# Imaginary column parts paired one frequency on, evictions of 642 columns on their own partition half, and a new order for the whole kernel

## The chip, the cores and the metric

One core of a Trainium2 chip. The time is device microseconds (us) of one execution, the median over several runs; the runs of one kernel agree within some tenths of a per cent. Of the kernel before, one execution was also taken by the hardware profiler, and all durations below come from it.

## The reference, cut to what matters

```python
xn = _layernorm(x, axis=-1)                 # x: 1 x 2048 x 640, bf16
# A: 2-D real Fourier transform, product with a filter W (2048 x 321), inverse transform
X = rfft2(xn, axes=(-2, -1)) * (w_r + 1j * w_i)
y = irfft2(X, s=(2048, 640)).astype(bf16)
# B: bilinear gated unit, 640 -> 1536 -> 640
h = (xn @ w_gate) * (xn @ w_up)
out = x + y + h @ w_down
```

## The kernel before, in words

Both branches run interleaved on one core. Work is cut into some 970 tasks, each a short list of instructions for one engine, and the order of all tasks is written out as a table, `_PLAN`: rows of (task number, engine, first PSUM bank or -1). `replay` walks the table, appends each task to its engine's list and adds, where a task takes PSUM banks, a dependence on the tasks that emptied those banks before. `compute_waits` turns dependences into semaphore waits. So each engine runs its list strictly in order, and nothing moves at run time. PSUM is eight banks of 512 f32 columns; a task takes a "single" bank or a "pair".

The stages, by the names that the tasks carry:

- **Layernorm** of 16 row groups (`bn`, `ag`, `sm`, `sq`, `sd`, `rs`, `mul`), and transposes: `T0` with evictions `eT0` for the first four groups, the DMA queue for the others.
- **Gated unit**: `GU_f_b_u` is five matmuls of 512 columns (line 940; smaller ones at line 960) for block f of 128 features, row group b, and u = gate or up. `eG` evicts the bank to bf16, mostly on ScalarE (ACT), and `H` multiplies the two on VectorE (DVE, line 976).
- **Forward transform along columns**: `S1` to `S5` on DVE (lines 852 to 887) do butterflies over five, `R_b` (line 900) the first factor along the 2048 rows, and `eR` evicts into buffer `U`, laid out as [contraction, part k, 2048] with column 64 q + m for row frequency q = 0 to 31.
- **D, C, WM, IA**, for t = 0 to 15, each t holding the frequencies q = 2t and 2t + 1. `D_t_w` (line 1017), w = 0 for the real and w = 1 for the imaginary part, is five matmuls of 64 or 65 columns with 128 columns of `U` as weights, so that PSUM partitions 0 to 63 hold q = 2t and 64 to 127 hold q = 2t + 1. `eD_t_w` copies the two halves, 64 partitions x 321 columns each, to `A[64 w + ..., slot, 324 g + ...]`, g = 0 or 1 for the two q: real parts in partitions 0 to 63 and imaginary parts in 64 to 127, so half of the copies change their partition half. `C_t` (line 1037) contracts over those 128 partitions with table `tf`; `WM_t` (six DVE instructions, lines 1054 and 1060) multiplies by the filter, `NS_t` on GpSimd (POOL) negates and copies a part, and for each odd t `SM_t` (lines 1081 and 1082), `JA_t` and `JB_t` (lines 1090 to 1093, on ACT or DVE) combine four frequencies. `IA_q` (lines 1108 and 1110) starts the inverse transform and `eIA_q` evicts it into `Z2`.
- **Inverse**: `I_a` (line 1139), `eI_a`, the butterflies `V1` to `V5` (lines 1163 to 1196), and `IV` (line 1228), which adds into the bank where `ACC` (line 1216) has summed h @ w_down. `FINA` on ACT and `FIN` on DVE add x, and the SP queue stores.

The first 68 us hold layernorm, S, most of R and a little over half of the gated unit; from 71 us D, C, WM and IA run between the rest of the gated unit; from 135 us I, V and the second product.

Buffer `A` has three slots (ar = t mod 3), buffer `Y5` three, `PR` two. All copies that ACT or DVE may do go through one helper, whose two lines the profile names for most of them: 683 (ACT) and 684 (DVE).

Of the kernel before, what the change touches and what calls it, by code (L numbers as in the profile page):

```python
# [255 lines left out]
def _build_tables():  # L256
# [66 lines left out]
    for q in range(_NQ):  # L323
        k = _rows(q, npm, nk1)
        ph = two_pi * ((s1[:, None] * k[None, :]) % _S) / _S
        c = np.exp(-1j * ph)
        pm = np.broadcast_to(npm[None, :], (64, 64))
        f = np.where(ck == 1, np.where(pm == 1, -1j, 1j), 1.0 + 0j)
        if q == 0:
            f = (ck == pm).astype(np.complex128)  # L330
        fm = c * f
        im = (np.conj(c) * f / _S).T
        tf[0:64, q, n_re] = fm.real
        tf[0:64, q, n_im] = fm.imag
        tf[64:128, q, n_re] = -fm.imag
        tf[64:128, q, n_im] = fm.real
        ti[n_re, q, 0] = im.real
        ti[n_im, q, 0] = -im.imag
        ti[n_re, q, 1] = im.imag
        ti[n_im, q, 1] = im.real  # L340
    t["tf"] = _bf16_bits(tf)
# [34 lines left out]
def _d_mm(n):  # L376
    return max(n, 64) / 2.4 + 2.5
# [22 lines left out]
def _d_act(n):  # L400
# [4 lines left out]
    (11, 4, -1), (0, 1, -1), (12, 4, -1), (170, 1, -1), (169, 4, -1), (18, 2, -1), (17, 2, -1), (171, 4, -1), (26, 2, -1),  # L405
    (10, 0, 0), (19, 2, -1), (8, 3, -1), (27, 2, -1), (20, 1, -1), (21, 2, -1), (172, 4, -1), (28, 2, -1), (22, 2, -1),
    (29, 1, -1), (23, 0, 2), (9, 0, 4), (13, 4, -1), (14, 4, -1), (30, 2, -1), (24, 1, -1), (31, 2, -1), (32, 0, 6),
    (33, 1, -1), (25, 2, -1), (173, 4, -1), (34, 2, -1), (181, 0, 5), (179, 0, 4), (189, 0, 0), (35, 2, -1), (174, 4, -1),
    (36, 2, -1), (37, 2, -1), (186, 0, 1), (184, 0, 2), (182, 1, -1), (191, 0, 3), (180, 1, -1), (183, 2, -1), (196, 0, 6),
    (194, 0, 7), (187, 2, -1), (175, 4, -1), (43, 1, -1), (38, 1, -1), (176, 4, -1), (15, 4, -1), (44, 1, -1), (39, 2, -1),  # L410
    (45, 1, -1), (185, 2, -1), (40, 2, -1), (177, 4, -1), (188, 2, -1), (41, 0, 1), (190, 1, -1), (46, 2, -1), (192, 1, -1),
    (42, 1, -1), (47, 2, -1), (193, 2, -1), (199, 0, 5), (195, 1, -1), (197, 1, -1), (178, 4, -1), (48, 0, 4), (112, 2, -1),
    (49, 1, -1), (200, 1, -1), (201, 0, 2), (202, 1, -1), (198, 2, -1), (113, 2, -1), (203, 2, -1), (1, 4, -1), (16, 4, -1),
    (204, 0, 0), (206, 0, 1), (205, 1, -1), (114, 2, -1), (62, 1, -1), (216, 0, 0), (207, 1, -1), (63, 1, -1), (50, 2, -1),
    (217, 1, -1), (54, 2, -1), (53, 2, -1), (51, 2, -1), (115, 2, -1), (64, 1, -1), (52, 2, -1), (55, 2, -1), (2, 4, -1),
    (211, 0, 3), (116, 2, -1), (56, 1, -1), (3, 4, -1), (57, 2, -1), (214, 0, 2), (209, 0, 7), (4, 4, -1), (208, 2, -1),
    (119, 0, 4), (65, 1, -1), (212, 1, -1), (221, 0, 6), (219, 0, 3), (66, 1, -1), (210, 1, -1), (58, 2, -1), (120, 1, -1),
    (60, 2, -1), (121, 2, -1), (215, 1, -1), (213, 2, -1), (222, 1, -1), (122, 2, -1), (117, 0, 0), (72, 1, -1), (218, 2, -1),
    (67, 2, -1), (220, 1, -1), (73, 1, -1), (5, 4, -1), (123, 2, -1), (224, 0, 7), (6, 4, -1), (225, 1, -1), (7, 4, -1),
    (74, 1, -1), (68, 2, -1), (226, 0, 4), (229, 0, 5), (223, 2, -1), (70, 2, -1), (231, 0, 2), (124, 2, -1), (227, 1, -1),  # L420
    (75, 1, -1), (236, 0, 3), (234, 0, 4), (76, 1, -1), (228, 2, -1), (230, 1, -1), (125, 2, -1), (239, 0, 5), (59, 4, -1),
    (61, 4, -1), (77, 2, -1), (78, 2, -1), (69, 4, -1), (232, 1, -1), (80, 2, -1), (82, 1, -1), (71, 4, -1), (241, 0, 2),
    (237, 1, -1), (235, 1, -1), (83, 1, -1), (240, 1, -1), (118, 1, -1), (84, 1, -1), (233, 2, -1), (246, 0, 3), (130, 2, -1),
    (126, 0, 6), (238, 2, -1), (251, 0, 4), (85, 1, -1), (128, 0, 0), (131, 2, -1), (242, 1, -1), (243, 2, -1), (79, 4, -1),
    (81, 4, -1), (431, 4, -1), (132, 2, -1), (432, 4, -1), (92, 1, -1), (244, 0, 5), (249, 0, 2), (247, 1, -1), (433, 4, -1),
    (93, 1, -1), (86, 1, -1), (87, 2, -1), (245, 1, -1), (252, 1, -1), (254, 0, 3), (248, 2, -1), (133, 2, -1), (256, 0, 5),
    (94, 1, -1), (250, 1, -1), (259, 0, 4), (95, 1, -1), (434, 4, -1), (253, 2, -1), (134, 2, -1), (261, 0, 2), (435, 4, -1),
    (129, 1, -1), (264, 0, 0), (96, 1, -1), (436, 4, -1), (90, 2, -1), (255, 1, -1), (437, 4, -1), (97, 2, -1), (257, 1, -1),
    (88, 2, -1), (102, 1, -1), (262, 1, -1), (98, 2, -1), (260, 1, -1), (265, 1, -1), (438, 4, -1), (266, 0, 1), (267, 1, -1),
    (258, 2, -1), (143, 2, -1), (269, 0, 3), (439, 4, -1), (263, 2, -1), (137, 0, 4), (127, 1, -1), (138, 1, -1), (103, 1, -1),  # L430
    (271, 0, 2), (139, 0, 0), (141, 0, 6), (274, 0, 4), (144, 2, -1), (272, 1, -1), (440, 4, -1), (276, 0, 5), (270, 1, -1),
    (268, 2, -1), (275, 1, -1), (135, 0, 2), (142, 1, -1), (100, 2, -1), (279, 0, 4), (104, 1, -1), (281, 0, 6), (273, 2, -1),
    (105, 1, -1), (145, 2, -1), (441, 4, -1), (277, 1, -1), (286, 0, 7), (284, 0, 5), (442, 4, -1), (106, 1, -1), (468, 4, -1),
    (469, 4, -1), (278, 2, -1), (470, 4, -1), (107, 2, -1), (282, 1, -1), (146, 2, -1), (291, 0, 6), (280, 1, -1), (140, 1, -1),
    (283, 2, -1), (147, 2, -1), (285, 1, -1), (294, 0, 4), (148, 0, 0), (89, 4, -1), (287, 1, -1), (289, 0, 5), (149, 1, -1),
    (296, 0, 7), (91, 4, -1), (99, 4, -1), (136, 1, -1), (110, 2, -1), (108, 2, -1), (292, 1, -1), (288, 2, -1), (101, 4, -1),
    (471, 4, -1), (150, 0, 0), (290, 1, -1), (472, 4, -1), (154, 0, 2), (156, 2, -1), (301, 0, 6), (295, 1, -1), (297, 1, -1),
    (299, 0, 7), (293, 2, -1), (473, 4, -1), (302, 1, -1), (151, 1, -1), (152, 0, 4), (474, 4, -1), (300, 1, -1), (157, 2, -1),
    (298, 2, -1), (475, 4, -1), (109, 4, -1), (155, 1, -1), (153, 1, -1), (304, 0, 6), (306, 0, 7), (311, 0, 0), (309, 0, 1),
    (158, 2, -1), (303, 2, -1), (314, 0, 2), (305, 1, -1), (310, 1, -1), (159, 2, -1), (307, 1, -1), (111, 4, -1), (160, 2, -1),  # L440
    (316, 0, 3), (308, 2, -1), (167, 0, 4), (161, 0, 6), (315, 1, -1), (312, 1, -1), (317, 1, -1), (429, 4, -1), (165, 0, 0),
    (313, 2, -1), (319, 0, 2), (430, 4, -1), (166, 1, -1), (318, 2, -1), (163, 0, 0), (321, 0, 3), (699, 4, -1), (162, 2, -1),
    (168, 1, -1), (320, 2, -1), (164, 1, -1), (445, 0, 2), (443, 0, 6), (501, 4, -1), (478, 0, 7), (446, 2, -1), (322, 1, -1),
    (452, 0, 4), (502, 4, -1), (450, 0, 5), (476, 0, 0), (453, 2, -1), (324, 0, 1), (444, 1, -1), (447, 0, 2), (503, 4, -1),
    (323, 2, -1), (451, 1, -1), (477, 1, -1), (326, 0, 6), (504, 4, -1), (454, 0, 4), (334, 0, 0), (325, 1, -1), (448, 2, -1),
    (505, 4, -1), (506, 4, -1), (485, 0, 1), (507, 4, -1), (455, 2, -1), (483, 0, 2), (327, 1, -1), (508, 4, -1), (457, 2, -1),
    (479, 1, -1), (335, 1, -1), (449, 3, -1), (486, 1, -1), (329, 0, 3), (328, 2, -1), (331, 0, 6), (534, 4, -1), (336, 0, 7),
    (480, 0, 4), (509, 0, 0), (459, 2, -1), (330, 1, -1), (341, 0, 1), (481, 2, -1), (535, 4, -1), (484, 1, -1), (332, 1, -1),
    (458, 1, -1), (337, 1, -1), (333, 2, -1), (460, 0, 3), (536, 4, -1), (510, 1, -1), (342, 1, -1), (462, 0, 2), (487, 0, 6),
    (339, 0, 4), (488, 2, -1), (456, 3, -1), (463, 1, -1), (461, 1, -1), (516, 0, 5), (511, 0, 0), (346, 0, 1), (518, 0, 2),  # L450
    (490, 2, -1), (338, 2, -1), (466, 0, 3), (464, 0, 6), (512, 1, -1), (340, 1, -1), (344, 0, 7), (347, 1, -1), (482, 3, -1),
    (465, 1, -1), (513, 0, 0), (467, 1, -1), (492, 2, -1), (491, 2, -1), (519, 1, -1), (489, 3, -1), (537, 4, -1), (514, 2, -1),
    (351, 0, 4), (495, 0, 6), (549, 0, 3), (538, 4, -1), (343, 2, -1), (517, 1, -1), (352, 1, -1), (349, 0, 2), (539, 4, -1),
# [69 lines left out]
def _build(nc, A_x, A_w_r, A_w_i, B_w_gate, B_w_up, B_w_down, out, opts=None):  # L523
# [3 lines left out]
    with es:  # L527
# [68 lines left out]
        def V(name):  # L596
            off, sz = lay[name]
            return arena[:, off: off + sz]
# [741 lines left out]
```

## Time and profile before

| | |
|---|---|
| median of 4 runs | 198.62 us (198.46 to 199.16) |
| the profiled execution's own time | 198.59 us |
| its span in the profile | 196.7 us; 1.9 us lie around it |
| PE (TensorE) busy | 191.0 us, 97%; weight loads 63% |
| DVE busy | 175.7 us, 89% |
| ACT busy | 138.5 us, 70% |
| POOL busy | 26.5 us, 13% |
| TensorE clock granted | full throughout |

How to read it: busy time of PE counts matmuls whose ends are modelled and overlap, so a sum of single durations is larger than the time they take; what a matmul costs in a stream is read from runs of them in the chain of waits. A group's idle time is that of its engine just before it, with the engine that ended it.

### The profile page before, as it was taken

To read this page: it belongs to the slowest core of one execution; us is meant where nothing else is said; L and a number is where in the kernel's file an instruction comes from. 1 tells how busy PE (TensorE), PEld (TensorE's weight loads), DVE (VectorE), ACT (ScalarE), POOL (GpSimd) and SP (SyncE) were. 2 spreads that over 40 slices of the span, in tenths; PEclk is the share of its full clock that TensorE was granted. 3 is DMA by queue.
4 is the path that set the end of the run, shared out by engine and by line. 5 is a ranking of instruction groups with operands and counts; after the bars stand their busy time and mean duration, and the time that the engine had idled before them with its cause. 6 is when DMAs were issued, how large, how long until landed. Compare 5 with 4: busy or idle time off the path is not lost.

```text
span 196.7 us, 4281 instructions
## 1 busy us (share of the span) xinstructions
PE 191.0 (97%) x1609; PEld 123.3 (63%) x1625; DVE 175.7 (89%) x390; ACT 138.5 (70%) x301; POOL 26.5 (13%) x53
## 2 busy tenths in 40 slices
PE   8899999999999999899999999999999999999995
PEld 8798644445454554455555555557777777777774
DVE  2599999999999979899998999995999999959953
ACT  2498999999878589999989999967414424323320
POOL 0000000000000004545332245460000000000000
PEclk9999999999999999999999999999999999999999
DMA  6999996524427432542452402003400334314422
GB/s 180 306 327 376 386 170 124 113 63 85 100 61 226 180 86 55 131 103 58 114 140 64 119 18 67 2 3 113 124 0 31 102 103 141 118 44 133 130 72 67
DMA packets 29667, 23.78 MB, mean 121 GB/s; under 512 B 10576, under 2 KB 27600, under 8 KB 29520
## 3 DMA queue, kind: packets, MB, share of 16 engines
q1 hardware_dynamic: 28848, 23.16, 43.1%
q10 hardware_dynamic: 800, 0.36, 0.6%
q8 instruction: 13, 0.21, 0.5%
q14 instruction: 6, 0.05, 0.1%
HBM read 18.92 MB, written 2.62 MB: 110 GB/s over the span
## 4 chain that ended last, share of the span: by engine, by line
PE 68%; DVE 16%; ACT 6%; issue 4%; DMA 3%; SPq 2%
PE ps L940 29%; PE ps L1216 27%; ACT arena L683 5%; DMA arena<-in_A_x_dram 3%; PE ps L1108 2%; PE ps L1139 2%; PE ps L1228 2%; DVE arena L853 2%; DVE arena L791 2%; PE ps L1037 2%; DVE arena L976 2%; PE ps L1017 2%; DVE arena L852 2%; SPq L677 2%; DVE arena L864 1%
## 5 line engine op out<-in xcount | busy, mean ns | idle before, releaser
L683 ACT ACTIVATE arena<-ps 128x512 bf16<-128x512 f32 (+6 forms) x244 | 117.8, 530 | 48.3 <-PE ps L1228 22.9
L940 PE MATMUL ps<-arena 128*128 128x512 bf16 x404 | 95.6, 379 | 0.9
L940 PEld LDWEIGHTS ps<-arena 128*128 128x128 bf16 x420 | 38.7, 98 | 39.0
L1216 PE MATMUL ps<-arena 128*128 128x320 bf16 (+2 forms) x396 | 57.4, 295 | 0.1
L1216 PEld LDWEIGHTS ps<-arena 128*128 128x128 bf16 x396 | 37.4, 98 | 13.7 <-issue 0.4
L1054 DVE TENSOR_TENSOR arena<-ps,arena 128x256 bf16<-128x256 f32 x64 | 22.6, 417 | 1.5 <-PE ps L1037 1.0
L1069 POOL COPY arena<-arena 128x126 bf16<-128x126 bf16 x16 | 7.6, 473 | 106.2 <-DVE arena L1060 106.2
L976 DVE TENSOR_TENSOR arena<-arena 128x512 bf16<-128x512 bf16 x42 | 17.9, 426 | 0.9 <-ACT arena L683 0.5
L960 PE MATMUL ps<-arena 128*128 128x128 bf16 (+1 forms) x160 | 13.7, 246 | 0.0
L960 PEld LDWEIGHTS ps<-arena 128*128 128x128 bf16 x160 | 12.2, 98 | 1.1 <-issue 0.2
L1255 DVE TENSOR_TENSOR arena<-arena 128x640 bf16<-128x640 bf16 x15 | 7.2, 487 | 5.8 <-ACT arena L683 5.6
L1071 POOL TENSOR_SCALAR arena<-arena 128x130 bf16<-128x130 bf16 x16 | 12.1, 758 | 0.0
L1108 PEld LDWEIGHTS ps<-arena 128*128 128x128 bf16 x128 | 8.2, 119 | 4.7 <-issue 1.1
L684 DVE CAST arena<-ps 64x321 bf16<-64x321 f32 (+4 forms) x17 | 9.1, 546 | 2.1 <-PE ps L1110 0.9
L1017 PEld LDWEIGHTS ps<-arena 128*128 128x128 bf16 x160 | 7.4, 98 | 3.6 <-issue 0.2
L1108 PE MATMUL ps<-arena 128*128 128x64 bf16 x128 | 8.6, 199 | 0.7 <-ACT arena L683 0.7
L741 ACT ACTIVATE arena<-arena 128x640 bf16<-128x640 bf16 x11 | 9.2, 834 | 0.1
L732 ACT ACTIVATE arena<-arena 128x640 bf16<-128x640 bf16 x11 | 8.2, 741 | 1.3 <-DMA arena<-in_A_x_dram 1.2
L750 DVE BATCH_NORM_STATS2 arena<-arena 128x6 f32<-128x320 bf16 x10 | 4.4, 479 | 5.1 <-DMA arena<-in_A_x_dram 5.1
L1017 PE MATMUL ps<-arena 128*128 128x64 bf16 (+1 forms) x160 | 8.3, 193 | 0.0
L1060 DVE TENSOR_TENSOR arena<-ps,arena 128x130 bf16<-128x130 f32 x32 | 7.9, 292 | 0.0
L852 DVE TENSOR_TENSOR arena<-arena 128x768 f32<-128x768 bf16 (+1 forms) x10 | 7.9, 789 | 0.0
(63 smaller groups left out, 203.8 us busy)
## 6 DMA issues: line engine op xcount, KB each, us to landing
arena<-in_A_x_dram SPq DMA_DIRECT2D x20, 160.0 KB, 2.7
arena<-in_A_w_r_dram SPq DMA_DIRECT2D x30, 80.2 KB, 2.2
arena<-in_A_w_i_dram SPq DMA_DIRECT2D x30, 80.2 KB, 2.3
out_dram<-arena SPq DMA_DIRECT2D x15, 160.0 KB, 1.8
arena<-in_B_w_gate_dram SPq DMA_DIRECT2D x4, 320.0 KB, 5.5
arena<-in_A_x_dram SPq DMA_DIRECT2D x1, 1280.0 KB, 9.9
arena<-c_tf SPq DMA_DIRECT2D x4, 256.0 KB, 10.1
arena<-c_ti SPq DMA_DIRECT2D x2, 512.0 KB, 5.6
```

Source lines behind the costliest of these rows:

```text
L683: return c.e.activation(dst, src, _ACTF.Copy)
L684: return c.e.tensor_copy(dst, src)
L741: return c.e.activation(v_jk, v_x[:, b, :], _ACTF.Square, scale=-1.0, bias=v_m32[:, b:b + 1], accum_out=v_ss[:, b:b + 1])
L852: c.e.tensor_tensor(uo[:, o, :, 0:3, :], v_xb[:, b:b + nt, 0:6:2, :], v_xb[:, b:b + nt, 5:10:2, :], op)
L940: ins = c.e.matmul(ps[:, bk, :], v_gw[:, w, j, ft, :], v_xt[:, j, rows], start=(j == 0), stop=(j == 4))
L960: ins = c.e.matmul(ps[:, bk, w * n:(w + 1) * n], v_gw[:, w, j, ft, :], v_xt[:, j, rows], start=(j == 0), stop=(j == 4))
L976: return c.e.tensor_tensor(v_ht[:, ft0, rows], v_gbf[:, rr, 0, :], v_gbf[:, rr, 1, :], _OP.mult)
L1017: ins = c.e.matmul(ps[:, bk, k * 64:k * 64 + n], v_uq[:, k, t, :], v_fd[:, k * 128 + w * n: k * 128 + w * n + n], start=True, stop=True)
L1054: c.e.tensor_tensor(dst, xh, wv, _OP.mult)
L1071: return c.e.tensor_scalar(yg[:, :, 128:193], yg[:, :, 256:321], -1.0, None, _OP.mult)
L1108: c.e.matmul(ps[:, bk, 64 * k:64 * k + 64], yl[:, k:512:4], v_ti[:, q, 0, :], start=True, stop=True)
L1216: ins = c.e.matmul(ps[:, bk, 0:sl3.stop - sl3.start], v_ht[:, ft, a * 128:(a + 1) * 128], v_wd[:, ft, sl3], start=(ft == _FT_ORDER[0]), st ...
```

## The change

It does three things.

1. D and eD. One task `D_t` replaces `D_t_0` and `D_t_1`. For the real part the weights are columns 128 t to 128 t + 127 of `U`, as before; for the imaginary part they start 64 columns later, so that PSUM partitions 0 to 63 hold the imaginary part of q = 2t + 1 and partitions 64 to 127 that of q = 2t + 2. The two parts lie in two neighbouring banks. `eD_t` is two copies of 2 x 321 columns in place of four of 321: partitions 0 to 63 of both banks go to partitions 0 to 63 of slot t mod 3 (real part of 2t, imaginary part of 2t + 1), and partitions 64 to 127 go to 64 to 127: the real part of 2t + 1 to this slot, the imaginary part of 2t + 2 to the next t's slot. One more task, `D_9`'s namesake made at t = 0 (called "first D" below: five matmuls and one copy of 321 columns), supplies the imaginary part of q = 0. At t = 15 the last copy has 321 columns.
2. Table `tf` has its partition halves exchanged for odd q, since there the imaginary part now lies in partitions 0 to 63.
3. `_PLAN` is a different order throughout (945 rows in place of 975). In it `D_t` and `D_t+1` stand close together for most even t, and some other tasks change the engine that they run on.

```diff
+    tf[:, 1::2] = np.concatenate([tf[64:128, 1::2], tf[0:64, 1::2]])
...
-            for w in range(2):
-                def em_d(c, t=t, w=w):
...
-                        ins = c.e.matmul(ps[:, bk, k * 64:k * 64 + n], v_uq[:, k, t, :],
-                                         v_fd[:, k * 128 + w * n: k * 128 + w * n + n], start=True, stop=True)
...
-                    for g in range(2):
-                        ins = copy_on(c, v_a[64 * w:64 * w + 64, ar, 324 * g:324 * g + 321],
-                                      ps[64 * g:64 * g + 64, bk, 0:321])
...
+            if t == 0:
+                def em_d9(c):
...
+                        o_ = lay["U"][0] + 2048 * k - 64
+                        ins = c.e.matmul(ps[:, bk, k * 64:k * 64 + n], arena[:, o_:o_ + 128],
+                                         v_fd[:, k * 128 + n: k * 128 + 2 * n], start=True, stop=True)
...
+                    return copy_on(c, v_a[64:128, 0, 0:321], ps[64:128, bank_of(td9), 0:321])
...
+            def em_d(c, t=t):
...
+                for w in range(2):
+                    m = 64 if w and t == 15 else 128
+                    for k in range(5):
...
+                        o_ = 128 * t + 64 * w
+                        ins = c.e.matmul(ps[0:m, bk + w, k * 64:k * 64 + n], v_uj[:, k, o_:o_ + m],
+                                         v_fd[:, k * 128 + w * n: k * 128 + w * n + n], start=True, stop=True)
...
+            def em_ed(c, td=td, ar=ar, an=an, t=t):
+                bk = bank_of(td)
+                copy_on(c, v_a[0:64, ar].rearrange("p (g n) -> p g n", g=2)[:, :, 0:321], ps[0:64, bk:bk + 2, 0:321])
+                if t == 15:
+                    return copy_on(c, v_a[64:128, ar, 324:645], ps[64:128, bk, 0:321])
+                o_ = 648 * ar + 324
+                if an:
+                    dst = V("A")[64:128, o_:o_ + 648].rearrange("p (g n) -> p g n", g=2)[:, :, 0:321]
+                else:
+                    dst = V("A")[64:128].rearrange("p (g n) -> p g n", g=6)[:, 5::-5, 0:321]
+                return copy_on(c, dst, ps[64:128, bk:bk + 2, 0:321])
```

The order of PE's tasks around the change, from the first D to the second product, before (part):

```
R_15 R_12 R_14 GU_2_8_0 R_13 GU_2_8_1 D_0_1 D_0_0 D_2_1 D_1_1 D_1_0 D_2_0 GU_3_8_0 C_0 GU_3_8_1 C_1 GU_5_8_0 D_3_1 D_3_0 GU_4_8_0
GU_4_8_1 GU_5_8_1 C_2 D_4_0 GU_6_8_1 IA_0 IA_1 C_3 ...
... IA_21 C_13 D_14_1 D_14_0 GU_9_12_1 IA_23 GU_8_12_1 D_15_1 D_15_0 GU_10_12_1 IA_22 C_14 GU_9_12_0 IA_24 IA_25 C_15 ACC_1_1
GU_11_12_1 IA_27 GU_10_12_0 IA_26 GU_11_12_0 ACC_0_0 IA_28 IA_31 IA_30 IA_29 ACC_0_0 I_0 ...
```

and after:

```
R_13 R_15 GU_3_8_0 R_12 R_14 GU_2_8_1 D_0 D_1 first_D GU_4_8_1 GU_2_8_0 C_0 GU_3_8_1 C_1 GU_4_8_0 D_2 D_3 GU_5_8_0 GU_5_8_1
GU_6_8_0 GU_7_8_0 C_2 GU_6_8_1 IA_1 GU_7_8_1 IA_0 D_4 C_3 D_5 ...
... GU_8_12_1 IA_20 IA_21 IA_22 C_13 IA_23 D_14 D_15 GU_9_12_1 GU_10_12_0 C_14 GU_10_12_1 IA_25 IA_24 C_15 GU_9_12_0 GU_11_12_0
IA_26 IA_27 GU_11_12_1 ACC_0_0 ACC_1_0 IA_30 IA_29 IA_31 IA_28 ACC_1_0 I_0 ...
```

Engines that tasks move to: eD, six copies on DVE before, two after (eD_0); eG, six on DVE before, four after; eR_15, and one of the eI more, to DVE; JA_1 and JB_7 from ACT to DVE, JB_13 from DVE to ACT.

## The prediction

> **What bounds the kernel now.** I read the busy rows first, then busy time by stage, then runs of matmuls in the chain of waits, and last the waits of PE.
>
> ```profile
> PE 191.0 (97%) x1609; PEld 123.3 (63%) x1625; DVE 175.7 (89%) x390; ACT 138.5 (70%) x301; POOL 26.5 (13%) x53
> ```
>
> The stages (columns: window, its length, then PE, weight loads, DVE, ACT and POOL busy; clock, DMA share, GB/s):
>
> ```profile
> 0.70:67.80 67.10, 65.79 (x487) 40.87 (x492) 62.10 (x141) 55.53 (x124) 0.10 (x1) 1.00 0.73 198
> 67.80:71.10 3.30, 3.25 (x30) 2.12 (x31) 2.49 (x5) 2.77 (x5) 0.00 (x0) 1.00 0.00 0
> 71.10:135.10 64.00, 62.72 (x599) 36.05 (x608) 59.58 (x158) 58.43 (x128) 26.23 (x48) 1.00 0.30 74
> 135.10:194.30 59.20, 59.17 (x496) 44.27 (x495) 51.19 (x87) 21.73 (x45) 0.00 (x0) 1.00 0.31 96
> 194.30:196.70 2.40, 0.12 (x3) 0.00 (x0) 0.29 (x1) 0.00 (x0) 0.00 (x0) 1.00 0.23 61
> ```
>
> Length less PE busy is what any edit can win from PE's idle time: 1.31 us up to 67.8, 0.05, 1.28 in the stage of D to IA, and 0.03 after it. Is PE's busy time real work? Two pieces of the chain say so (start, length):
>
> ```profile
> 61.46 6.47 PE ps L940 x30
> 143.12 5.57 PE ps L1216 x41
> ```
>
> 6.47 / 30 is 216 ns for 512 columns and 5.57 / 41 is 136 ns for 320: matmuls run back to back at a price set by their columns. The kernel is bound by TensorE nearly throughout, and the change takes no matmul away. ACT and DVE are each over 90% busy from 71 to 135 us, but they cost time only where PE waits for them. PE's waits there:
>
> ```profile
> PEld ps L1108 <- issue: 1.1, 1, 1.1
> ...
> PEld ps L1216 <- issue: 0.4, 1, 0.4
> PEld ps L1139 <- issue: 0.3, 1, 0.3
> ```
>
> From matmul start to matmul start, less the price of the first, these and C_15's are 0.81 us (IA_0 at 81.6, behind JA_1 on ACT, which ended at 81.13), 0.13 (C_15, behind eD_15_0), 0.27 (ACC_1_1, whose bank eIA_24 empties) and 0.19 (I_0, behind the last eIA): 1.40 us.
>
> **What the Trainium skill says.** "TensorE: Matmul & The Clock Gate", section Back-to-back issue gap, gives N/2.4 + 2.5 ns: 216 for 512 columns, as here; its lower sustained figure of 131 ns doesn't appear. "ScalarE: Activation LUTs", section What ACT_TABLE_LOAD costs, gives a copy 186 ns + 0.833 ns per column, and an overlap of 93 ns between neighbours. The trace has 602 for 512 (estimate 612) and 434 for 321 (estimate 453). "VectorE: DVE Perf Modes", section Two Vector instructions with no wait between them, says that an instruction starts only after all earlier ones have finished when its input or output starts in another group of 32 partitions than the last. It says so of VectorE; the trace shows ACT alike: eD_0_0's two copies took 71.81 to 72.68, twice 434 with no overlap, where neighbouring evictions of 320 columns start 330 ns apart.
>
> **The change, part by part.**
>
> *PE.* D has ten matmuls a t as before. The first D adds five; 30 D matmuls at 71.1 us start 29 ns apart, so +0.15 us, and nothing hides it.
>
> *eD on ACT.* Row before:
>
> ```profile
> L683 ACT ACTIVATE arena<-ps 64x321 bf16<-64x321 f32 x58 | 25.2, 434 | 1.0 <-PE ps L1017 0.2
> ```
>
> No row has 642 columns on 64 partitions. From below: 434 + 321 x 0.833 = 701 ns; the nearest row, 128x640, has 717; from above, if two banks cost like two copies, 868. I take 710 and no overlap: 1.42 us for an eD. After: 29 copies of 642 and two of 321 on ACT, 29 x 0.71 + 0.87 = 21.5 us, against 25.2. With the moves (two more eG on ACT, +1.2; eR_15, an eI and one JA or JB fewer, -2.5) ACT loses 5 us of work; DVE loses 6 x 0.49 of eD, gains 2 x 0.82 (its 128x640 row has 818 ns), and with the moves (two eG, -1.4; eR_15, an eI and one JA or JB, +2.1) loses 0.6. All of it lies beside PE. It is worth only those of the 1.40 us that wait for ACT.
>
> *The order up to D.* T0_0 comes earlier: ag0 stands ahead of bn1_0 on DVE, so mul0 ends about 5.4 for 5.94. But GU_1_0 waits for eT0_0 on ACT, behind sd_1, and its weights land at 6.57; I get 6.8, and GU_0_1, now behind T0_1's evictions, 8.4 for 8.26. mul2 stands behind H_1 on DVE: T0_2 at 12.05 for 11.67. So PE is 0.3 us late at 15 us. Cover: R_13 can't start before S5_4 on DVE (67.69 before; DVE's list up to it holds the same work), and before, PE waited some 0.25 us for DVE between 33 and 67.8. Net 0, and up to +0.3 without that cover. D_0 stays at 71.1.
>
> *D to C_13.* I went through PE's new list with measured times (GU 1.08, IA 0.19, C 0.27, D 0.29; an evictor starts about 0.2 after the last matmul; WM 1.82, SM 1.39, JA or JB on DVE 0.42). D_0 71.1; C_0 74.0, with eD_0 done on DVE at 73.6 and eD_1 on ACT at 73.9; IA_1 at 83.0, its JB_1, now on DVE, done at 81.9. So the 0.81 us goes. WM_2 runs at 82.1, 2.2 us later than before, but DVE's list from WM_3 to JB_15 is 3.3 us shorter, so the later chains meet their readers. The tightest bank is GU_2_12_1's, behind eIA_9: PE has 0.85 us of work between (D_8, C_7, D_9), the eviction needs 0.2 + 0.43 + 0.1.
>
> *C_13 to I_0.* Here new waits come. IA_25 needs JB_13, now on ACT, behind SM_13 on DVE. Chain from C_13's first matmul: 0.47 to WM_13, 1.83, H_45 0.33, SM_13 1.42, JB_13 1.08, 0.08: 5.2 us. PE's work up to IA_25: C_13, IA_23, D_14, D_15, three GU and C_14: 0.27 + 0.19 + 0.58 + 3.24 + 0.27 = 4.55. Wait 0.65 (0.45 of it may show at D_15, whose bank eIA_23 empties). Queued behind JB_13 on ACT is eG_47_1, which frees C_15's banks: 0.6 more, less IA_25 and IA_24: 0.23. I_0 keeps 0.19, since ACC_1_0's four matmuls, 0.54, again are all that covers the last eIA. The end of JB_15's chain has 0.2 us of cover at IA_30. New waits: 1.07.
>
> *I_0 to the end.* The same matmuls; V1_0 and IV_0 stand as far behind I_0 as before (13.3 us against 13.4 of PE work), the tail is the same: 0.
>
> **Sum:** -1.40 + 1.07 + 0.15 = -0.18 us on the span of 196.7; the profiled execution's 198.59 (1.9 around the span) becomes 198.4, and against the median of 198.62, 0.03 above it, the change is the same 0.1%.
>
> **The rivals.**
>
> *Faster: the new waits at IA_25 and C_15 don't come,* as a chain on DVE runs earlier than I have it. For it: DVE loses 0.6 and ACT 5 us of work. Against: the C_13 chain starts at PE's own C_13. Then -1.40 + 0.19 + 0.15 = -1.06: 197.5.
>
> *Slower: banks.* Two D in a row take four of eight banks, and their eD keep ACT for 2.84 us in one piece; evictions queue behind and GU waits for a bank. For it: of PE's waits from 64 to 134 us, those with under 1.1 us of PE work in PE's order between the matmul whose result is evicted and the task that waits for that rise from 3 to 7, I_0 apart (GU_9_8_0 1.05, GU_2_12_1 0.85, D_15 0.29 among them). It decides from 1.6 us per eD on: PE's list has some 3.2 us (three GU) behind most pairs. At 868 ns a copy an eD is 1.74, and 0.25 us lost at six pairs gives +1.5 on my sum: 199.9.
>
> *The copies don't get cheaper at all.* Then ACT has 26 us of eD rather than 21.5 in a stage where PE still has more: if banks hold, 198.4 to 198.8.
>
> **How the numbers follow.** A measurement of this kernel can tell about 0.3% (0.6 us) from no change. The sum near zero, cheap copies or not: 0.43, own range 198.0 to 199.2. Faster: 0.28. Slower by banks or by waits in a wholly new order that I didn't see: 0.29. PE's idle time caps the gain at some 1.9 us, so the low end is 197.5; the high end of 199.8 takes in most of the bank case.
>
> **What would show it.** Right: PE busy near 191.2; no PE wait at IA_0 or IA_1; waits of 0.4 to 0.7 at IA_25 or D_15, 0.2 at C_15 and I_0; the 64x642 row at 700 to 720 ns; ACT near 134 busy. Wrong: copies over 800 ns; PE idle in the D stage above 2 us or under 0.6; R_13 later than 68.1.

## The result, and the profile after

| | before | after |
|---|---|---|
| median | 198.6 us (198.26 to 199.84, 64 runs) | 199.29 us (198.83 to 200.97, 43 runs) |
| ratio, after to before | | 1.0033, 95% interval 1.0025 to 1.0041 |
| profiled execution: its own time | 198.59 | 199.34 |
| its span | 196.7 | 196.8 |
| time less span | 1.9 | 2.5 |

By the ratio the changed kernel is 0.66 us slower. The last two rows say where: the span, from the first to the last instruction, is as long as before to within 0.1 us. The loss lies outside it, and in every run: the median of time less span is 2.52 us over all runs of the kernel after and 1.88 over 53 runs of the kernel before.

The busy row of the kernel after (engine, us, share of the span, instructions):

```profile
PE 191.1 (97%) x1613; PEld 123.5 (63%) x1630; DVE 175.3 (89%) x387; ACT 133.4 (68%) x273; POOL 28.2 (14%) x53
```

Stages (window, its length, then PE, weight loads, DVE, ACT and POOL busy; clock, DMA share, GB/s):

```profile
0.70:67.80 67.10, 65.65 (x488) 40.88 (x494) 62.40 (x141) 55.96 (x124) 0.10 (x1) 1.00 0.77 198
67.80:71.10 3.30, 3.25 (x33) 2.12 (x33) 2.45 (x5) 2.45 (x4) 0.00 (x0) 1.00 0.00 0
71.10:135.10 64.00, 62.86 (x603) 36.27 (x612) 57.87 (x154) 53.89 (x101) 27.93 (x48) 1.00 0.30 74
135.10:194.30 59.20, 59.17 (x496) 44.27 (x495) 52.26 (x88) 21.13 (x45) 0.00 (x0) 1.00 0.31 95
194.30:196.80 2.50, 0.19 (x4) 0.01 (x1) 0.29 (x1) 0.00 (x0) 0.00 (x0) 1.00 0.24 65
```

From 71.1 to 135.1 us ACT has lost 4.5 us of work and DVE 1.7, and PE's part is the same: 62.86 of 64 us for 62.72. Runs of matmuls in the chain of waits give 216 ns for 512 columns (8.63 / 40) and 136 for 320 (5.98 / 44), as before:

```profile
59.29 8.63 PE ps L938 x40
142.78 5.98 PE ps L1240 x44
```

ACT's copies of 642 columns, by shape (busy us, mean ns), and the waits of weight loads from 71 to 136 us (us in total, times, longest):

```profile
L681 ACT ACTIVATE arena<-ps 64x642 bf16<-64x642 f32 x29 | 20.4, 702 | 0.3
```

```profile
PEld ps L1061 <- issue: 0.6, 1, 0.6
PEld ps L1036 <- ACT arena L681: 0.4, 1, 0.4
PEld ps L938 <- ACT arena L681: 0.4, 1, 0.4
PEld ps L1163 <- issue: 0.3, 1, 0.3
```

IA's line (L1132) has no long wait any more; D_15 (L1036), C_14 (L1061), GU_9_12_0 (L938) and I_0 (L1163) have. Nothing here makes the kernel slower. What is outside the span shows when the DMA view is asked for the time behind its end, 196.9 to 200.5 us, in 40 slices of 0.09 us. Before:

```profile
DMA  0000000003000000000000000000000000000000
...
q14 instruction: 1, 0.01, 0.8%
```

and after:

```profile
DMA  0000000000000000000000030000000000000000
...
q14 instruction: 1, 0.01, 0.9%
```

One packet each, a fetch of instructions: 1.0 us after the span's end before the change, 2.3 us after it now. (At 64 bytes an instruction, q8's 13 pieces of 16 KiB within the span are 3328 instructions, which fits PE's 3333 and 3340 below; q14, with 8192 bytes a packet, is taken to serve the others.) So the suspicion fell on the engines' instruction streams, whose lengths the change alters. In instructions of 64 bytes, waits counted too, the compiled kernels have: ACT 326 before and 296 after, DVE 450 and 447, PE 3333 and 3340, POOL 69 and SP 158 in both. The page's own counts give DVE's difference as well: x390 and x387.

### The profile page after: what moved, and what is told of

The parts are those of the page before. It is cut to its first block, busy times and chain, and to the rows that moved or that the text cites. A ratio compares the mean times of both kernels' runs of the same rounds, so it can differ in the third digit from the quotient of the medians.

```text
span 196.8 us, 4254 instructions
## 1 busy us (share of the span) xinstructions
PE 191.1 (97%) x1613; PEld 123.5 (63%) x1630; DVE 175.3 (89%) x387; ACT 133.4 (68%) x273; POOL 28.2 (14%) x53
## 4 chain that ended last, share of the span: by engine, by line
PE 73%; ACT 17%; SPq 4%; DMA 4%; issue 1%; DVE 0%
PE ps L938 34%; PE ps L1240 27%; ACT arena L681 10%; SPq L675 4%; DMA arena<-in_A_x_dram 4%; ACT arena L730 3%; ACT arena L739 3%; PE ps L1163 2%; PE ps L1252 2%; PE ps L1061 2%; PE ps L1036 2%; PE ps L1132 2%; PE ps L898 2%; PE ps L1134 1%; ACT arena L764 0%
## 5 line engine op out<-in xcount | busy, mean ns | idle before, releaser
L681 ACT ACTIVATE arena<-ps 128x512 bf16<-128x512 f32 (+6 forms) x217 | 114.2, 579 | 53.2 <-PE ps L1252 22.5
L938 PE MATMUL ps<-arena 128*128 128x512 bf16 x403 | 95.0, 379 | 1.1 <-issue 0.2
L938 PEld LDWEIGHTS ps<-arena 128*128 128x128 bf16 x420 | 39.1, 98 | 40.9 <-ACT arena L681 0.8
L1240 PE MATMUL ps<-arena 128*128 128x320 bf16 (+2 forms) x396 | 57.3, 295 | 0.0
L1240 PEld LDWEIGHTS ps<-arena 128*128 128x128 bf16 x396 | 37.5, 98 | 13.3
L1093 POOL COPY arena<-arena 128x126 bf16<-128x126 bf16 x16 | 7.7, 480 | 104.5 <-DVE arena L1084 104.5
L958 PEld LDWEIGHTS ps<-arena 128*128 128x128 bf16 x160 | 12.3, 98 | 1.6 <-DMA arena<-in_B_w_gate_dram 0.6
L1095 POOL TENSOR_SCALAR arena<-arena 128x130 bf16<-128x130 bf16 x16 | 13.1, 820 | 0.0
L1132 PEld LDWEIGHTS ps<-arena 128*128 128x128 bf16 x128 | 8.3, 119 | 3.8 <-ACT arena L681 0.2
L1132 PE MATMUL ps<-arena 128*128 128x64 bf16 x128 | 8.5, 199 | 0.0
L1094 POOL COPY arena<-arena 128x126 bf16<-128x126 bf16 x16 | 8.5, 529 | 0.0
L682 DVE CAST arena<-ps 128x320 bf16<-128x320 f32 (+4 forms) x12 | 7.1, 619 | 1.5 <-PE ps L898 0.8
L1252 PE MATMUL ps<-arena 128*128 128x320 bf16 (+2 forms) x33 | 7.6, 295 | 0.0
```

The source lines that it names most:

```text
L681: return c.e.activation(dst, src, _ACTF.Copy)
L938: ins = c.e.matmul(ps[:, bk, :], v_gw[:, w, j, ft, :], v_xt[:, j, rows], start=(j == 0), stop=(j == 4))
L958: ins = c.e.matmul(ps[:, bk, w * n:(w + 1) * n], v_gw[:, w, j, ft, :], v_xt[:, j, rows], start=(j == 0), stop=(j == 4))
L1094: c.e.tensor_copy(yg[:, :, 193:256], yg[:, :, 1:64])
L1095: return c.e.tensor_scalar(yg[:, :, 128:193], yg[:, :, 256:321], -1.0, None, _OP.mult)
L1132: c.e.matmul(ps[:, bk, 64 * k:64 * k + 64], yl[:, k:512:4], v_ti[:, q, 0, :], start=True, stop=True)
```

## The experiments

Time less span is the number to read in the first group. It is the median over a kernel's runs; every ratio is to the kernel before on the same chip. The padding is nearly always this, with tiny instructions that nothing waits for, on columns that nothing else uses:

```diff
                 for t in sch.order[ename]:
+                    for _ in range(pads.get(t.name, 0)):
...
+                        if ename == "act":
+                            eng.activation(v_pad, v_one[0:32, 0:1], _ACTF.Copy)
+                        else:
+                            eng.memset(v_pad, 0.0)
                     for (dm, val) in t.waits:
```

### Which stream: ACT, DVE or PE

```diff
+        pads = {'FINA_8_0': 15, 'FINA_14_1': 15}
```

> The changed kernel with 30 one-column copies added to ACT late in its list (15 in its idle time at 172.6 us, 15 at 188.8), which gives ACT as many instructions as in the kernel before (326 in its stream instead of 296). They touch one unused column and nothing waits for them. The span of the profiled executions was 196.7 before and 196.8 after, but the time less the span 1.9 before and 2.5 after. Theory A (the instruction fetch at the end of ACT's stream lies outside the span since ACT has fewer instructions): the time returns to that of the kernel before, ratio 1.000, time less span 1.9, last instruction fetch about 1.0 us after the span's end. Theory D (the same by DVE's stream), theory P (by PE's), and the theory that the 0.65 us belongs to work within the span: ratio 1.003, time less span 2.5, last fetch 2.3 us after the end.

```diff
+        pads = {'FIN_14': 3}
```

> The changed kernel with 3 one-column memsets added on DVE ahead of FIN_14, where DVE is idle, so that DVE's stream is as long as before (450 instructions instead of 447). Theory D: ratio to the kernel before 1.000 and time less span 1.9. Theories A, P and that of work within the span: ratio 1.003, time less span 2.5.

```diff
-            for i in range(4 * nwarm):
+            for i in range(36):
```

> The changed kernel with 36 of the 40 warm-up matmuls ahead of T0_0, which are done before the first data come: PE's stream has 3332 instructions instead of 3340 (3333 in the kernel before). Theory P: ratio to the kernel before 1.000 and time less span 1.9. The other theories: ratio 1.003, time less span 2.5.

The three edits together:

> The three edits together: ACT 326, DVE 450 and PE 3332 instructions, as in the kernel before to within one, with the changed kernel's order and tiles untouched. If the time outside the span is a matter of stream lengths at all: ratio to the kernel before 1.000 (1.3 us at most less than the span's difference allows), time less span 1.9. If it is something else (the new order's last transfers, its waits, or chance): ratio 1.003, time less span 2.5.

| | ACT / DVE / PE | span, median | time less span | ratio, 95% interval |
|---|---|---|---|---|
| 30 on ACT | 326 / 447 / 3340 | 196.80 | 2.47 | 1.0029 [1.0017, 1.0042] |
| 3 on DVE | 296 / 450 / 3340 | 196.75 | 1.86 | 0.9991 [0.9976, 1.0005] |
| 8 fewer on PE | 296 / 447 / 3332 | 197.45 | 2.53 | 1.0055 [1.0033, 1.0076] |
| all three | 326 / 450 / 3332 | 197.80 | 1.87 | 1.0036 [1.0020, 1.0051] |

Three memsets on DVE, in idle time at 189 us, take the whole loss back; 30 copies on ACT and the shorter stream of PE do not. The DMA view behind the span's end, of the run with 30 on ACT (196.9 to 200.0, slices of 0.08 us) and of the one with 3 on DVE (196.9 to 200.5), shows which fetch is whose:

```profile
DMA  0000000000300000000000000040000000000000
...
q14 instruction: 2, 0.02, 2.1%
```

```profile
DMA packets 0, 0.00 MB, mean 0 GB/s; under 512 B 0, under 2 KB 0, under 8 KB 0
```

With ACT at 326 there is a fetch 1.0 us behind the end, and it costs nothing (2.47 against 2.52). With DVE at 447 there is one 2.3 us behind the end; with 450 it is gone, and 0.65 us with it. In the trace of all three edits only the fetch at 1.0 us is left.

The ratio of "all three" missed its expectation although its time less span is as forecast: its span is 1 us longer. The longer span comes from a slow start of PE. In the trace of the kernel with 8 fewer on PE, the first matmuls of 128 columns start 107 ns apart instead of 56 up to 9.3 us. Two windows of it (x12 matmuls in a us)

```profile
7.00:8.00 1.00, 1.00 (x12) 1.00 (x11) 0.09 (x1) 0.00 (x0) 0.00 (x0) 1.00 1.16 306
8.00:9.00 1.00, 1.00 (x12) 1.00 (x11) 0.36 (x1) 0.36 (x1) 0.00 (x0) 1.00 1.11 339
```

and the same two with all 40 warm-up matmuls, from the run with 3 on DVE:

```profile
7.00:8.00 1.00, 1.00 (x20) 1.00 (x19) 0.12 (x2) 0.08 (x1) 0.00 (x0) 1.00 1.15 302
8.00:9.00 1.00, 1.00 (x19) 0.87 (x17) 0.28 (x1) 0.83 (x3) 0.00 (x0) 1.00 1.11 340
```

PE is busy throughout in both; it just runs at half pace. Fewer warm-up matmuls make this frequent, but they neither suffice for it nor are they needed: the traced execution of "all three" (36 matmuls) runs at full pace and has a span of 196.7, and that of the kernel before with DVE at 447, below (40 matmuls), runs at half pace up to 9.5 us and has 197.6. A span of 197.3 or more has 13 of 53 runs of the kernel before, and 21 of the 30 runs with 36 matmuls.

### Is it DVE's length in the kernel before as well, and which lengths?

```diff
             def em_v1(c, gr=gr, nt=nt, n=n):
...
+                if c.t.name == "V1_14":
+                    return c.e.scalar_tensor_tensor(v_vt[:, 3, 0:n], b1i, _RT, b2i, _OP.mult, _OP.subtract)
```

> The kernel before with DVE's stream cut from 450 to 447 instructions, as long as the changed kernel's: three of the four operations of V1_14 (at 180 us, where PE waits for nothing) are left out, so that part of the inverse transform isn't computed. Nothing else is touched. Theory D (the length of DVE's stream sets the time outside the span, whatever else the kernel holds): span 196.7 as before, time less span 2.5, ratio 1.003. Rival (the 2.5 belongs to the new order or the new tiles, and the three memsets of the run with 450 helped in another way): time less span 1.9, ratio 1.000.

The changed kernel with DVE at 448 (one memset ahead of FIN_14), 511 and 575:

```diff
+        pads = {'FIN_14': 1}
+        pads = {'bn0_1': 24, 'FIN_14': 40}
+        pads = {'bn0_1': 36, 'FIN_14': 54, 'FIN_13': 12, 'FIN_7': 7, 'FIN_10': 6, 'FIN_12': 6, 'FIN_15_1': 7}
```

> The changed kernel with one memset added on DVE instead of three: 448 instructions in its stream. Its fetches are of 8192 bytes, 128 instructions, and 448 is three and a half such pieces. If the edge lies at a half piece and 448 is past it: time less span 1.9, ratio 1.000. If it lies at 449 or 450, or depends on more than the count: time less span 2.5, ratio 1.003.

> The changed kernel with 64 memsets of one column on DVE (24 before the first data, 40 ahead of FIN_14): 511 instructions in its stream, 64 more than the 447 of the slower closing. They lie in idle time of DVE, so the span should stay within 0.2 us of 196.8. If the closing depends on the stream's length modulo 64: time less span 2.5. If only on the length modulo 128, or if every stream of 450 or more closes early: 1.9.

> The same with 128 memsets more, 575 instructions on DVE, spread over its idle time; the span may grow by some tenths. If the closing depends on the length modulo 128 (one fetch of 8192 bytes) or modulo 64: time less span 2.5. If every stream of 450 or more closes early: 1.9.

| | DVE | span, median | time less span | ratio, 95% interval |
|---|---|---|---|---|
| before, V1_14 cut | 447 | 196.70 | 2.53 | 1.0033 [1.0020, 1.0046] |
| after, 1 more | 448 | 196.80 | 2.60 | 1.0035 [1.0022, 1.0049] |
| after, 64 more | 511 | 197.10 | 1.81 | 1.0014 [1.0001, 1.0027] |
| after, 128 more | 575 | 201.75 | 2.58 | 1.0276 [1.0237, 1.0314] |

The kernel before, with its own order and its own tiles, gets exactly the changed kernel's loss when three DVE instructions are taken from it. The edge lies between 448 and 450. 511 closes early and 575 = 447 + 128 closes late: that fits a period of 128 instructions, one fetch of 8192 bytes, and neither a period of 64 nor "every stream of 450 or more". (There are only two runs with 575, and their span is 5 us longer where some tenths were expected: the memsets ahead of the first data delay the start, the granted clock is shown as 0.50 from 7 to 10 us, and those ahead of FIN_14 still run at 198.7. The time less span is read beside that. With 511 the span is 0.3 us longer, 0.2 at most expected.) The late fetch is there again at 575, 2.4 us behind the end at 201.5 (window 201.6 to 204.6, slices of 0.075 us):

```profile
DMA  0000000000000000000000000000003000000000
...
q14 instruction: 1, 0.01, 0.9%
```

The distance of this fetch from the span's end and the time less span go together in every trace that has it: 2.26 to 2.32 us and 2.5 to 2.6 in five kernels with 447, 448 or 575. The trace of the kernel with 8 fewer on PE has DVE at 447 and no such fetch, and that one execution closed at 2.1 us, the other seven of its kernel at 2.5 to 2.6. (7 runs of the changed kernel lie at 2.1 to 2.2, too.)

What isn't shown is which instruction waits. If all the time outside lies behind the span, the late fetch begins some 0.2 to 0.3 us ahead of the end of the measured time, and the trace has no DVE instruction there. So the fetch marks the late closing; that DVE stalls for it is an inference.

### What the eD copies are worth

With DVE at 450, so that the closing is the early one, each copy of 642 columns is split in two, first in the order half 0, half 0, half 1, half 1, then with the halves in turn:

```diff
             def em_ed(c, td=td, ar=ar, an=an, t=t):
                 bk = bank_of(td)
+                def copy_on(c, dst, src):
...
+                    for g in range(2):
+                        ins = copy_on(c, dst[:, g], src[:, g])
+                    return ins
```

> The changed kernel with every eD of 642 columns written as two copies of 321 per half, as it would be without the new pairing; DVE padded to 450 instructions, so that the time outside the span is 1.9. An eD on ACT is then 4 x 434 = 1.74 us instead of 1.41, and ACT has 5 us more of work. The prediction's rival of banks: waits behind the evictions at some six pairs, span 198.2 (1.5 more), time 200.1. Theory of the prediction (banks hold, DVE's chain and not ACT sets the stage from C_12 on): span 196.8 to 197.2, time 198.7 to 199.1.

```diff
+                    for x in [y for z in zip(todo[0:2], todo[2:4]) for y in z] + todo[1:2] * (len(todo) == 3):
+                        ins = copy_half(c, *x)
```

> As the run with two copies of 321 per half, but with the halves taken in turn, as before the change: DVE padded to 450. If ACT overlaps two copies only where they keep their half, the run before it had 1.52 us an eD because its order kept the half twice, and an eD is now 4 x 0.44 = 1.75 us; ACT has 5 us more of copies than in the changed kernel. If ACT sets the end of any wait of PE, the span grows from 196.8 by up to 0.5, and by the prediction's rival of banks by 1.5; if DVE's chain sets them, the span stays at 196.8 to 197.0 and the time at 198.7 to 198.9.

| | an eD on ACT | span, median | ratio, 95% interval |
|---|---|---|---|
| copies of 642 (3 on DVE) | 1.41 | 196.75 | 0.9991 [0.9976, 1.0005] |
| copies of 321, half kept twice | 1.52 | 196.85 | 1.0007 [0.9997, 1.0017] |
| copies of 321, halves in turn | 1.74 | 198.75 | 1.0092 [1.0072, 1.0113] |

ACT's rows by shape, of the second kernel and of the third:

```profile
L1047 ACT ACTIVATE arena<-ps 64x321 bf16<-64x321 f32 x59 | 22.4, 430 | 0.3
```

```profile
L681 ACT ACTIVATE arena<-ps 64x321 bf16<-64x321 f32 x59 | 25.7, 435 | 0.7
```

The same 59 copies of the same mean duration keep ACT busy for 22.4 us in one order and 25.7 in the other: neighbours that keep their half start some 330 ns apart, and across halves 446. The bank isn't what decides: in the first order neighbours of one half read two different banks, in the second neighbours of one bank change the half and start 433 to 450 ns apart. The wider copy by itself saves 0.11 us of ACT an eD, which the time doesn't show (the two intervals overlap); keeping the half saves 0.22. The first kernel missed its expectation of 1.74 us for an eD, which had priced the split and overlooked the order; the second hit it. And its price is steep: from 1.52 to 1.74 us an eD the span grows by 1.9. The waits of weight loads from 71 to 136 us in that kernel:

```profile
PEld ps L1079 <- issue: 1.3, 3, 0.6
PEld ps L1041 <- ACT arena L686: 1.0, 2, 0.5
PEld ps L1150 <- ACT arena L686: 0.9, 2, 0.6
PEld ps L1150 <- issue: 0.8, 2, 0.5
PEld ps L1150 <- ACT arena L1134: 0.6, 1, 0.6
```

C (L1079), D (L1041) and IA (L1150) wait ten times, 4.6 us in all. All lines of this view together are 5.7 us, against 2.5 in the kernel that keeps the half. Five of the ten waits are traced to ACT. The four behind L686 are for evictions that empty banks, as the prediction's rival of banks has it; the one behind L1134 is for a JB, and what C and two of the IA wait for ("issue") the view doesn't say. So the rival's late ACT is shown, and banks as a part of its cost.

### Who sets the end of the stage

```diff
-    (629, 2, -1), (419, 0, 6), (413, 2, -1), (606, 1, -1),
-    (630, 2, -1), (631, 1, -1), (650, 0, 4),
+    (629, 2, -1), (631, 2, -1), (419, 0, 6), (413, 2, -1), (606, 1, -1),
+    (630, 2, -1), (650, 0, 4),
```

> The changed kernel with JB_13 back on DVE right behind SM_13 (0.42 us there instead of 1.08 on ACT), DVE padded to 450. The prediction made JB_13 on ACT responsible for a new wait of 0.65 us at IA_25: by it IA_25 can start 0.7 us earlier and up to 0.6 us of the span goes, span 196.1, time 198.0. Rival, from the trace of the kernel after (PE waits at D_15 for eIA_23, at C_14 for SM_13, at GU_9_12_0 for eIA_25, and not at IA_25; DVE runs without a pause from WM_12 at 120.8 us to JB_15 at 133.15, which IA_30 needs at 133.57): H_46, JA_13 and both WM behind it come 0.45 us later, and the span grows by 0.1 to 0.4: 196.9 to 197.2, time 198.8 to 199.1.

Measured: span 196.95, time 198.81, ratio 1.0010 [0.9998, 1.0021]; 0.2 us longer than with JB_13 on ACT (196.75), where up to 0.6 less was the other forecast. The rival was right: DVE runs without a pause from WM_12 to JB_15, which ends at 133.5 where the changed kernel has 133.15, and IA's weight loads, which had one such wait of 0.2 us, now have two with 0.6 (one of them ahead of IA_30):

```profile
PEld ps L1132 <- issue: 0.6, 2, 0.4
```

The kernel before with JA_1 on DVE:

```diff
-    (480, 0, 4), (509, 0, 0), (459, 2, -1), (330, 1, -1),
+    (480, 0, 4), (509, 0, 0), (459, 2, -1), (458, 2, -1), (330, 1, -1),
```

> The kernel before with one task moved: JA_1 from ACT (80.07 to 81.13 us) to DVE, right behind JB_1, 0.42 us there. DVE has 451 instructions, so the time outside the span stays 1.9. The prediction gave 0.81 us to IA_0's wait for JA_1. IA_0 can then start at 80.8. If PE's gain lasts to the end: span 195.9, time 197.8, ratio 0.996. If DVE's chain from WM_2 to JB_15, which starts 0.42 us later and has some 1.2 us of pauses to take that up, sets IA_28 at 133.5 again: span 196.4 to 196.8, time 198.3 to 198.7, ratio 0.998 to 1.000.

Measured: span 196.80, time 198.84, ratio 1.0012 [0.9994, 1.0030]. IA_0's wait goes as expected (it starts at 80.98), and comes back at once. PE's timeline (start, length, line; in brackets the idle time and what ended it):

```profile
80.98 0.30 PE L1108 MATMUL ps<-arena 128*128 128x64 bf16 x4
...
82.63 1.03 PE L940 MATMUL ps<-arena 128*128 128x512 bf16 x4 [0.83 <-DVE arena L1060]
```

GU_6_8_0, next but two on PE, needs the banks that WM_2 empties, and WM_2 now stands behind JA_1 on DVE. The wait was turned into another within 2 us. (Time less span is 2.05 here with DVE at 451, 0.17 more than in the runs with 450, where 1.9 was expected. The trace has an instruction fetch 1.8 us behind the span's end that those with 450 lack; why it comes at that place isn't known.)

Last, the D stage's remaining losses in the changed kernel, DVE at 450:

```diff
-                    m = 64 if w and t == 15 else 128
+                    m = 128
```

> The changed kernel with the last five matmuls of D_15 using 128 weight columns instead of 64 (the 64 more give rows of PSUM that nothing reads); DVE padded to 450. In the traces of the changed kernel the first of those five and the matmul behind the last start 125 and 130 ns after the one in front, where D's matmuls follow after 29: 0.2 us that the prediction's sum doesn't have. Theory S (this is the term by which the span came out 0.25 us above the sum): span 196.55, time 198.4, ratio 0.999. Rival (C_14, 2.3 us later on PE, waits for SM_13 on DVE anyway and swallows it): C_14's wait grows from 0.26 to 0.45, span 196.75, time 198.6, ratio 1.000.

and with C_14 (650) moved behind GU_10_12_1 (421):

```diff
-    (630, 2, -1), (631, 1, -1), (650, 0, 4), (628, 3, -1), (421, 0, 7),
+    (630, 2, -1), (631, 1, -1), (628, 3, -1), (421, 0, 7), (650, 0, 4),
```

> The same with C_14 moved behind GU_10_12_1 on PE, whose 1.08 us cover its wait for SM_13. If PE's order sets the end of this stage: C_14's wait of 0.26 and the 0.2 of D_15 go, span 196.3 to 196.5, time 198.2 to 198.4, ratio 0.998. If DVE's chain sets it: C_14 comes some 0.6 us later, WM_14 on DVE starts up to 0.3 us later than at 127.26, JB_15 ends that much later than 133.15, and IA_30 waits for it: span 196.7 to 196.9, ratio 1.000 to 1.001.

Measured: span 196.60, ratio 1.0003 [0.9994, 1.0011]; and span 196.80, ratio 1.0005 [0.9994, 1.0016]. PE's timelines from D_14 to C_14, of the kernel with 3 on DVE

```profile
122.64 0.46 PE L1036 MATMUL ps<-arena 128*128 128x64 bf16 x10
123.40 0.59 PE L1036 MATMUL ps<-arena 128*128 128x64 bf16 x10 [0.30 <-ACT arena L681]
123.93 2.33 PE L938 MATMUL ps<-arena 128*128 128x512 bf16 x10
126.36 0.43 PE L1061 MATMUL ps<-arena 128*128 128x321 bf16 x2
```

and of the one with D_15 wide:

```profile
122.49 0.46 PE L1036 MATMUL ps<-arena 128*128 128x64 bf16 x10
123.26 0.47 PE L1036 MATMUL ps<-arena 128*128 128x64 bf16 x10 [0.31 <-ACT arena L681]
123.78 2.18 PE L938 MATMUL ps<-arena 128*128 128x512 bf16 x9
126.22 0.43 PE L1061 MATMUL ps<-arena 128*128 128x321 bf16 x2 [0.26 <-ACT arena L681]
```

D_15 itself is shorter (0.47 for 0.59), but from D_14 to C_14 it is 3.72 us in the one and 3.73 in the other: C_14 waits for SM_13 and swallows it. (In the second trace the record of the first GU matmul behind D_15 is missing. The bracket at C_14 names ACT, which ended an eviction last; by the kernel's own waits C_14 needs of ACT only eD_14, done by 124.5, and of DVE SM_13, which ended at 126.07.) The median span of 196.60 alone would fit a gain of 0.15 us, but the 0.15 us by which the second trace is ahead was there before D_14. From D_14 to I_0 the two take 12.49 and 12.50 us, and with C_14 later 12.60. No edit of PE's side in this stretch gains anything, and no version here is clearly faster than the kernel before. Those with DVE at 450, all 40 warm-up matmuls and copies that keep their half equal it.

## Why the prediction was right and wrong

**Wrong: the time around the span.** The step is the last sentence of its sum, "the profiled execution's 198.59 (1.9 around the span) becomes 198.4": the 1.9 was carried over as a constant, and it was 2.5. The span was forecast at 196.5 and came out at 196.8; with 1.9 around it the result would have been 198.7, no change. DVE's length, 447 for 450, could have been counted ahead of any run, but nothing in the trace of before said that three instructions can cost 0.65 us at the close. The experiments show that they do, in both directions and in both kernels. That 199.29 lies within the stated 197.5 to 199.8 is luck: the upper end was there for bank waits, and these didn't come.

**Right: copies and busy times.** A copy of 642 columns takes 702 ns (710 taken), an eD 1.41 us (1.42), ACT is busy 133.4 us (near 134) and PE 191.1 (191.2). By matmul starts, D_0 came at 71.04 us, C_0 at 73.94, IA_1 at 82.90 with no wait (71.1, 74.0, 83.0 forecast), and R_13 at 67.76.

**Right: the waits that go.** By matmul starts, 0.81 us at IA_0, 0.13 at C_15 and 0.27 at ACC_1_1 are gone, and 0.19 at I_0 stayed. The start is 0.2 us worse (T0_2 at 11.94 us for 11.72), 0.3 forecast, and the cover that was named took it: before, PE lost 0.26 us to waits between 33 and 69 us, and in the changed kernel none of them is left.

**Partly wrong: the waits that come.** Forecast 0.65 at IA_25 or D_15 and 0.23 at C_15, 0.88 in all. Measured: 0.47 at D_15 behind eIA_23, 0.26 at C_14, 0.22 behind C_15 (at GU_9_12_0, for eIA_25), and 0.22 that are no wait but D_15's narrow weights: the first matmul with 64 weight columns came 125 ns after the one in front of it and the next GU 130 ns after the last, for 29. Together 1.17, 0.29 more than forecast, which is nearly all of the difference between the forecast -0.18 from D_0 to I_0 and the +0.14 found there. The step that failed is the chain "C_13's first matmul to IA_25, 5.2 us against 4.55 of PE's work". A tighter one ends earlier: C_14, which the forecast counts as work without a wait, waits for SM_13 too, because the program holds C_14 back until WM_14 may overwrite what SM_13 reads. From C_13's first matmul at 122.26 past SM_13's end at 126.31 to C_14 at 126.46 is 4.20 us, against 3.2 of PE's work (IA_23, C_13, D_14, D_15, two GU), so about 1 us is lost up to C_14, however it is spread over D_15, its narrow weights and C_14's own wait; the run with D_15 wide shows that taking one part away makes another grow. JB_13 on ACT, which the forecast blamed, ends ahead of IA_25, and moving it to DVE gained nothing.

**The rivals.** "Slower by banks" didn't happen, but it is real, and its point of decision was well placed: "from 1.6 us per eD on" it was said, and between 1.52 and 1.74 us the span grows by 1.9 (1.5 forecast), though not by banks alone. "Faster", with no new waits, fell with the chain to SM_13. "The copies don't get cheaper" fell with 702 ns.

**On ACT's overlap** the prediction carried a rule over from VectorE: the Trainium skill, "VectorE: DVE Perf Modes", section Two Vector instructions with no wait between them, says that an instruction that starts in another group of 32 partitions than the last waits for all earlier ones. The two kernels with split copies show it of ACT by measurement: 22.4 against 25.7 us for the same 59 copies.

## What to carry to other kernels

Split the time into span and what lies around it before explaining a difference under a per cent: 0.65 us here went with no wait within the span and no tile, but with the length of DVE's instruction stream, and three idle memsets took them back. A wait of PE is worth what the next chain behind it leaves: taking one away (JA_1, D_15's narrow weights) only moved it to the next task that waits for the same DVE chain, so follow the chain of the busier engine through the stage and not PE's waits one by one. For copies between partition halves, order them so that neighbours stay in one half; that was worth more than making them wider.

## What the runs showed of the hardware

- The time around the span depended on the number of DVE's instructions: 2.5 to 2.6 us at 447, 448 and 575, 1.8 to 1.9 at 450 and 511 (2.05 at 451). In the traces with an instruction fetch 1.8 to 2.3 us behind the span's end it is 0.2 to 0.3 us more than that distance. The lengths of ACT's (296 and 326) and PE's stream (3332 and 3340) made no difference.
- Within and behind the span, instruction fetches on q14 are of 8192 bytes and those on q8, by their number PE's, of 16 KiB. The Trainium skill, "Runtime: NRT & Kernel Launch", section Instruction fetch mechanics, says that engines fetch in blocks of 16 KiB while they run and that crossing into the next is mostly hidden. Within the span the traces agree, at 8192 bytes on q14: none of PE's waits named above is put down to a fetch. The late closing comes in behind the span, at the end of the stream, which the section doesn't speak of.
- ACT's neighbouring copies of 64 x 321 started some 330 ns apart when they kept their partition half and some 446 when they changed it, whichever bank they read.
- A change from 128 to 64 weight columns and back cost PE 0.1 us each way, at the one place that has it (D_15).
- In some executions PE ran at half pace (107 ns for 128 columns) up to 9.3 or 9.5 us, and the kernel was 1 us longer. It was seen with 36 and with 40 warm-up matmuls; spans of that size were 21 of 30 runs with 36 and 13 of 53 with 40.
